# Moving the spatial bias of a gated unit from TensorE to VectorE, and reordering the unit's stages

## The chip, the core and the metric

The kernel runs on one core of one Trainium2 chip. The metric is device time in microseconds (us) of one execution. A core has five engines that run side by side, each through its own queue in order: TensorE (PE, matmuls; its weight loads are shown as PEld), VectorE (DVE), ScalarE (ACT), GpSimd (POOL) and SyncE (SP, which here only issues DMAs). Matmul results land in PSUM, everything else lies in SBUF.

## The reference

Attention with grouped heads, whose output x goes straight into a gated MLP with a spatial projection (batch B = 8, sequence S = 384, 16 query heads on 4 key/value heads, D = 64, model width 1024, d_ff 1024):

```python
attn = softmax(scale * q @ k.T)                  # per head, 384 x 384
x = (attn @ v).transpose(0, 2, 1, 3).reshape(B, S, 1024)
h = np.maximum(x @ w_in, 0.0)
u, v = h[..., :512], h[..., 512:]
v_n = (v - mean(v)) / np.sqrt(var(v) + 1e-06)    # over the 512 features
v_s = np.einsum('ts,bsd->btd', w_spatial, v_n) + b_spatial[None, :, None]
gated = u * v_s
out = (gated @ w_out).astype(np.float32)
```

## The kernel before

**Two streams on TensorE.** The program is written out in steps n, 18 for each batch (`NU = 18`: six units of a query tile and half of the heads, by three key tiles), by a loop over `range(total + 6)`. In each step the loop emits attention work first: `scores(n)` (two pairs of matmuls on a 64-row half each, then one Exp of 128x1024 by ACT; from step 18 on two steps' scores are emitted together at even n) and, in two steps out of three, `weigh(b, m, hh)` (12 small matmuls against v into the PSUM tile `av`, of which there is one buffer, then a reciprocal and a product by DVE, which free it). Then `run_fill(cols)` emits so many matmul columns of the gated unit of an earlier batch. `gated_unit(b)` is a generator that yields the columns of each matmul; it starts at step 18(b+1)+2. So the unit of one batch lies between the attention matmuls of the next, and what is left of the last batch's unit comes alone at the end, the tail.

**The gated unit, in order** (before): three tiles of v (token tile st; `pv` at L322, 8 matmuls of 512 columns; then DVE: relu to `vr` L332, statistics L334, L335); four blocks of u transposed (`pu` at L369, 8 matmuls of 384 columns, relu to `uT` by ACT at L377); the normalisation in two parts (`normal(0)` after block 0: ACT Ln and Exp, L343 and L344, give `rstd`; `normal(1)` after block 1: DVE makes `nmr` at L346 and POOL the three `vn` at L351); four gates (`psp`, m = 0 to 3: one matmul of a vector of ones with the bias at L383, three against the spatial weights at L386, then DVE multiplies PSUM with `uT` into `gT` at L394); then the projection (`po` at L401, 24 matmuls of 512 columns, copied out by DVE and ACT in turn at L410, and stored by SP at L412 and L414). Batch 0 computes u by token tile instead (L303, L312), since its x arrives tile by tile.

**The bias** is a row in fp16 and a second row with its rounding rest, both in `bias_b`, which `prep_spatial` fills on POOL (L431 to L433).

**Buffers and queues.** All PSUM tiles `pv`, `pu`, `psp`, `po` and the transposes share three buffers (`ps_ck`, tag "ck"). POOL's queue holds, in program order, the casts of the k, q and v of a later batch (L159, L175, L164; steps 6 and 7 of a batch's 18, for batches 3 and up) and the `vn`. SP's queue holds loads, transposing DMAs of k, q and x (`x_turn`, L284) and stores. At the start `keep_warm` (L471) puts matmuls without use on TensorE while inputs arrive.

```python
        for m in range(NM):
            psp = ps_ck.tile([P, 512], FP32, name=f"psp_{b}_{m}", tag="ck")
            nc.tensor.matmul(psp[:, 0:S], ones_b, bias_b, start=True, stop=False)
...
            nc.vector.tensor_tensor(gT[:, m, :], psp[:, 0:S], uT[:, m, :], ALU.mult)
```

Of the kernel before, what the change touches and what calls it, by code (L numbers as in the profile page):

```python
# [9 lines left out]
FP32 = mybir.dt.float32  # L10
# [7 lines left out]
def kernel(  # L18
# [125 lines left out]
    ones_b = cst.tile([P, P], FP16, name="ones_b")  # L144
    nc.gpsimd.memset(ones_b, 0.0)
    nc.gpsimd.memset(ones_b[0:1, :], 1.0)
    nc.gpsimd.memset(ones_b[32:33, :], 1.0)
    bias_b = cst.tile([P, S], FP16, name="bias_b")
    nc.gpsimd.memset(bias_b, 0.0)
# [121 lines left out]
    def x_tile(b):  # L271
        if b not in xts:
            xts[b] = att.tile([P, NT, NB, P], FP16, name=f"xt_{b}", tag="xt")
        return xts[b]
# [15 lines left out]


    def gated_unit(b):
        xt = x_tile(b)
        last = b == B - 1
        mv = small.tile([P, NT, 2], FP32, name=f"mv_{b}", tag="mv")
        v_r, v_n = [], []
        uT = moe.tile([P, NM, S], FP16, name=f"uT_{b}", tag="uT")

        def u_tile(st):
            pu = ps_ck.tile([P, NM, P], FP32, name=f"pu_{b}_{st}", tag="ck")  # L300
            for m in range(NM):
                for kt in range(NB):
                    nc.tensor.matmul(  # L303
                        pu[:, m],
                        w_in16[:, kt, m * P : (m + 1) * P],
                        xt[:, st, kt],
                        start=(kt == 0),
                        stop=(kt == NB - 1),
                    )
                    if m < NM - 1 or kt < NB - 1:  # L310
                        yield P
            nc.vector.tensor_scalar(  # L312
                uT[:, :, st * P : (st + 1) * P], pu, 0.0, None, op0=ALU.max
            )
            yield P

        for st in range(NT):
            if st == 2 and b == 0:
                yield from u_tile(0)
            pv = ps_ck.tile([P, 512], FP32, name=f"pv_{b}_{st}", tag="ck")  # L320
            for kt in range(NB):
                nc.tensor.matmul(  # L322
                    pv,
                    xt[:, st, kt],
                    w_in16[:, kt, DH:DFF],
                    start=(kt == 0),
                    stop=(kt == NB - 1),
                )
                if kt < NB - 1:
                    yield 512  # L330
            vr = moe.tile([P, DH], FP32, name=f"vr_{b}_{st}", tag="vr", bufs=4)
            nc.vector.tensor_scalar(vr, pv, 0.0, None, op0=ALU.max)  # L332
            stats = small.tile([P, 6], FP32, name=f"stats_{b}_{st}", tag="stats")
            nc.vector.bn_stats(stats, vr)  # L334
            nc.vector.bn_aggr(mv[:, st, :], stats)  # L335
            v_r.append(vr)
            yield 512
        rstd = small.tile([P, NT], FP32, name=f"rstd_{b}", tag="rstd")
        nmr = small.tile([P, NT], FP32, name=f"nmr_{b}", tag="nmr")

        def normal(part):
            if part == 0:
                nc.scalar.activation(rstd, mv[:, :, 1], AF.Ln, bias=eps_t)  # L343
                nc.scalar.activation(rstd, rstd, AF.Exp, scale=-0.5)  # L344
                return
            nc.vector.scalar_tensor_tensor(  # L346
                nmr, mv[:, :, 0], -1.0, rstd, op0=ALU.mult, op1=ALU.mult
            )
            for st in range(NT):
                vn = moe.tile([P, DH], FP16, name=f"vn_{b}_{st}", tag="vn", bufs=6)  # L350
                nc.gpsimd.tensor_scalar(  # L351
                    vn,
                    v_r[st],
                    rstd[:, st : st + 1],
                    nmr[:, st : st + 1],
                    op0=ALU.mult,
                    op1=ALU.add,
                )
                v_n.append(vn)

        if b == 0:
            normal(0)
            normal(1)
            for st in (1, 2):
                yield from u_tile(st)
        for m in range(NM if b else 0):
            pu = ps_ck.tile([P, 512], FP32, name=f"pu_{b}_{m}", tag="ck")
            for kt in range(NB):
                nc.tensor.matmul(  # L369
                    pu[:, 0:S].rearrange("p (t s) -> p t s", t=NT),  # L370
                    w_in16[:, kt, m * P : (m + 1) * P],
                    xt[:, :, kt],
                    start=(kt == 0),
                    stop=(kt == NB - 1),
                )
                yield S
            nc.scalar.activation(uT[:, m, :], pu[:, 0:S], AF.Relu)  # L377
            if m < 2:
                normal(m)
        gT = moe.tile([P, NM, S], FP16, name=f"gT_{b}", tag="gT")  # L380
        for m in range(NM):
            psp = ps_ck.tile([P, 512], FP32, name=f"psp_{b}_{m}", tag="ck")
            nc.tensor.matmul(psp[:, 0:S], ones_b, bias_b, start=True, stop=False)  # L383
            yield S
            for st in range(NT):
                nc.tensor.matmul(  # L386
                    psp[:, 0:S],
                    v_n[st][:, m * P : (m + 1) * P],
                    wsT16[:, st, :],
                    start=False,  # L390
                    stop=(st == NT - 1),
                )
                yield S
            nc.vector.tensor_tensor(gT[:, m, :], psp[:, 0:S], uT[:, m, :], ALU.mult)  # L394
        rows = out[b].rearrange("(p t) d -> p t d", t=NT)
        for tt in range(NT):
            osb = ops.tile([P, DM], FP32, name=f"osb_{b}_{tt}", tag="osb")
            for half in range(2):
                po = ps_ck.tile([P, 512], FP32, name=f"po_{b}_{tt}_{half}", tag="ck")
                for m in range(NM):  # L400
                    nc.tensor.matmul(  # L401
                        po,
                        gT[:, m, tt * P : (tt + 1) * P],
                        w_out16[:, m, half * 512 : (half + 1) * 512],
                        start=(m == 0),
                        stop=(m == NM - 1),
                    )
                    yield 512
                cols = slice(half * 512, (half + 1) * 512)
                (nc.scalar.copy if half else nc.vector.tensor_copy)(osb[:, cols], po)  # L410
                if last:
                    nc.sync.dma_start(rows[:, tt, cols], osb[:, cols])  # L412
            if not last:
                nc.sync.dma_start(rows[:, tt, :], osb)  # L414

    HV = NB * 512
    COLS = NT * HV + NM * NB * S + NM * (NT + 1) * S + NT * 2 * NM * 512
# [4 lines left out]
    b32 = cst.tile([1, S], FP32, name="b32")  # L422

    def load_b():
        pool.dma_start(b32, moe_b_spatial.rearrange("(a s) -> a s", a=1))

    def prep_spatial():
        lo32 = cst.tile([1, S], FP32, name="lo32")
        bp = b32.rearrange("a (p t) -> a t p", t=NT)
        hi = bias_b[0:1, :].rearrange("a (t p) -> a t p", t=NT)  # L430
        nc.gpsimd.tensor_copy(hi, bp)  # L431
        nc.gpsimd.tensor_tensor(lo32.rearrange("a (t p) -> a t p", t=NT), bp, hi, ALU.subtract)
        nc.gpsimd.tensor_copy(bias_b[32:33, :], lo32)  # L433
# [27 lines left out]
    def turn_at(n, f, *args):  # L461

        turns.setdefault(n, []).append((f, args))
# [9 lines left out]
    keep_warm(24)  # L473
# [3 lines left out]
    keep_warm(8)  # L477
    q_transposes(0, 0, 0, by_act, by_dve)
    keep_warm(4)
# [19 lines left out]
    turn_at(0, q_transposes, 0, 1, 0, by_dve)  # L499
# [51 lines left out]
    fill = []  # L551
# [3 lines left out]
    def run_fill(cols):  # L555
        nonlocal owed
        owed = owed + cols if fill else 0.0
        while fill and owed > 0:
            try:
                owed -= next(fill[0])  # L560
            except StopIteration:
                fill.pop(0)

    early = 0
    for n in range(total + 6):
# [13 lines left out]
        if n == 10:  # L579
            fill.append(gated_unit(0))  # L580
        if n >= 2 * NU + 2 and (n - 2) % NU == 0 and (n - 2) // NU <= B:
            fill.append(gated_unit((n - 2) // NU - 1))
        if n < NU + 3:

            c = HV / 4 if 10 <= n < 14 else 2 * HV / 5 if 16 <= n else 0
            early += c
            run_fill(c)
        else:
            run_fill((COLS - (early if n < 2 * NU + 2 else 0)) / (NU if n >= 2 * NU + 2 else NU - 1))
    for g in fill:  # L590
        for _ in g:
            pass
# [29 lines left out]
```

## Time and profile before

| what | value |
|---|---|
| time, median of 3 runs (lowest to highest) | 255.3 us (254.73 to 255.41) |
| the profiled execution's own time | 255.16 us |
| its span (first to last instruction) | 253.1 us |
| what lies around the span | 2.06 us |
| granted TensorE clock | 1.0 |
| pv, 192 matmuls, share of the chain that ended last | 17% |
| pu in blocks, 224 matmuls | 15% |
| psp with the spatial weights, 96 matmuls | 6% |
| psp with the bias, 32 matmuls | 2% |
| POOL, busy per batch while casts run | 7.24 us |
| DVE, busy per batch | 15.9 us |
| ACT, busy per batch | 20.7 us |

The profile's busy time of a matmul overlaps the next one's, so that what a matmul costs is read from the chain of waits, which follows the last instruction back to what released it. "Busy per batch" is from windows of one period of the steady stage.

### The profile page before, as it was taken

Reading aid. Unit: us, or ns where it says so; the run is one execution under the profiler, and the core shown is the slowest. Engines: PE = TensorE matmul, PEld = TensorE weight load, DVE = VectorE, ACT = ScalarE, POOL = GpSimd, SP = SyncE. Lnnn points to the kernel's source line nnn. Section 1 sums busy time; section 2 is a strip of 40 time slices with the busy share of each in tenths; the row PEclk is TensorE's granted clock in tenths of the full one; section 3 lists DMA queues with packets and bytes.
Section 4 is the critical chain, followed back from the end, with each engine's and each line's share of the span. In section 5 each row is a group of like instructions: output and inputs, shape, how many; then the busy total and the mean of one; then the engine's idle time right before and its main releaser. Section 6 shows DMA issues by size and latency. Waiting matters only on the chain.

```text
span 253.1 us, 5997 instructions
## 1 busy us (share of the span) xinstructions
PE 244.7 (97%) x2457; PEld 129.1 (51%) x2457; DVE 140.1 (55%) x365; ACT 167.5 (66%) x215; POOL 75.0 (30%) x118
## 2 busy tenths in 40 slices
PE   7998998999999999999999999999999999999993
PEld 6564657534455445544455445544455445554541
DVE  2455776755727465455727465455727465465541
ACT  3896566687686867777686867777686867761311
POOL 4698857721032500261033400451030000200200
PEclk9999999999999999999999999999999999999999
DMA  7999997999179952999299962999174442025006
GB/s 182 266 290 246 285 301 195 313 217 271 65 143 311 270 182 54 201 304 252 98 137 298 248 223 57 236 279 280 60 145 96 139 153 41 3 67 223 3 22 227
DMA packets 73803, 46.71 MB, mean 185 GB/s; under 512 B 48113, under 2 KB 68657, under 8 KB 73777
## 3 DMA queue, kind: packets, MB, share of 16 engines
q1 hardware_dynamic: 68688, 37.63, 59.7%
q0 software_dynamic: 4048, 8.46, 13.5%
q8 instruction: 19, 0.31, 0.5%
q10 hardware_dynamic: 1040, 0.26, 0.5%
q14 instruction: 8, 0.06, 0.1%
HBM read 25.76 MB, written 12.58 MB: 151 GB/s over the span
## 4 chain that ended last, share of the span: by engine, by line
PE 91%; DVE 4%; ACT 2%; issue 1%; POOL 0%; DVEq 0%; POOLq 0%
PE pv L322 17%; PE av L252 16%; PE po L401 15%; PE sc L238 15%; PE pu L369 15%; PE psp L386 6%; PE warm L471 3%; PE psp L383 2%; ACT aT L245 1%; PE pu L303 1%; DVE x L264 1%; PE qps L205 1%; DVE gT L394 1%; DVE stats L334 1%; PE xps L280 1%
## 5 line engine op out<-in xcount | busy, mean ns | idle before, releaser
L245 ACT ACTIVATE aT<-sc 128x1024 f16<-128x1024 f32 x144 | 139.5, 1022 | 55.8 <-PE sc L238 55.6
L252 PEld LDWEIGHTS <-aT 128*128 128x128 f16 x1152 | 43.9, 97 | 29.1 <-DVE vr L332 5.7
L262 DVE RECIPROCAL r<-av 128x4 f32<-128x4 f32 x96 | 17.1, 178 | 67.2 <-PE av L252 67.2
L351 POOL TENSOR_SCALAR vn<-vr,rstd,nmr 128x512 f16<-128x512 f32 x24 | 18.1, 767 | 117.2 <-DVE nmr L346 90.7
L252 PE MATMUL av<-v,aT 128*128 128x65 f16 x1152 | 52.1, 194 | 0.5 <-DVE x L264 0.5
L401 PE MATMUL po<-w_out,gT 128*128 128x512 f16 x192 | 47.9, 379 | 0.4 <-ACT osb L410 0.3
L322 PE MATMUL pv<-w_in,xt 128*128 128x512 f16 x192 | 47.0, 379 | 0.2 <-DVE osb L410 0.2
L238 PE MATMUL sc<-qT,kT 64*128 64x512 f16 x288 | 45.4, 385 | 0.4 <-ACT aT L245 0.2
L264 DVE TENSOR_TENSOR x<-av,r 128x256 f16<-128x256 f32 x96 | 40.7, 424 | 3.3
L369 PE MATMUL pu<-xt,w_in 128*128 128x384 f16 x224 | 41.5, 326 | 0.0
L175 POOL CAST q<-q 128x768 f16<-128x768 f32 (+1 forms) x36 | 25.2, 732 | 15.3 <-DMA q<-in_q_dram 10.0
L369 PEld LDWEIGHTS <-w_in 128*128 128x128 f16 x224 | 20.2, 98 | 13.7 <-issue 2.5
L322 PEld LDWEIGHTS <-xt 128*128 128x128 f16 x192 | 16.6, 97 | 18.0 <-issue 1.9
L401 PEld LDWEIGHTS <-gT 128*128 128x128 f16 x192 | 16.5, 97 | 16.3 <-DVE gT L394 2.2
L394 DVE TENSOR_TENSOR gT<-psp,uT 128x384 f16<-128x384 f32 x32 | 17.7, 556 | 9.9 <-PE psp L386 9.2
L238 PEld LDWEIGHTS <-kT 64*128 64x128 f16 x288 | 9.1, 94 | 26.4 <-issue 24.5
L410 ACT COPY osb<-po 128x512 f32<-128x512 f32 x24 | 14.1, 589 | 12.1 <-PE po L401 12.0
L386 PE MATMUL psp<-wsT,vn 128*128 128x384 f16 x96 | 22.0, 326 | 0.0
L332 DVE TENSOR_SCALAR vr<-pv 128x512 f32<-128x512 f32 x24 | 16.6, 691 | 9.0 <-PE pv L322 8.3
L410 DVE COPY osb<-po 128x512 f32<-128x512 f32 x24 | 16.5, 688 | 6.4 <-PE po L401 6.3
L377 ACT ACTIVATE uT<-pu 128x384 f16<-128x384 f32 x28 | 13.8, 492 | 8.4 <-PE pu L369 8.4
L334 DVE BATCH_NORM_STATS2 stats<-vr 128x6 f32<-128x512 f32 x24 | 16.7, 695 | 0.8
(55 smaller groups left out, 127.8 us busy)
## 6 DMA issues: line engine op xcount, KB each, us to landing
out_dram<-osb SPq DMA_DIRECT2D x21, 512.0 KB, 3.8
q<-in_q_dram SPq DMA_DIRECT2D x10, 768.0 KB, 6.9
q<-in_q_dram POOLq DMA_DIRECT2D x4, 768.0 KB, 10.1
v<-in_v_dram SPq DMA_DIRECT2D x6, 384.0 KB, 8.3
w_in<-in_moe_w_in_dram POOLq DMA_DIRECT2D x4, 512.0 KB, 9.7
k<-in_k_dram SPq DMA_DIRECT2D x5, 384.0 KB, 4.1
out_dram<-osb SPq DMA_DIRECT2D x6, 256.0 KB, 2.0
q<-in_q_dram SPq DMA_DIRECT2D x2, 512.0 KB, 7.0
```

What stands on the lines that cost most here:

```text
L175: f(q16s[b, j][:, lo:hi, :, hh, :], src[:, hh, lo:hi])
L238: nc.tensor.matmul(sc[:, hh], kTs[b][half, j, t * P : (t + 1) * P], qTs[b, j][half, qt], start=True, stop=True,)
L245: nc.scalar.activation(aTs[b, m][:, t], sc, AF.Exp, scale=scale)
L252: nc.tensor.matmul(av[:, i, :], aTs[b, m][:, t, hh, i * P : (i + 1) * P], v1[b % 2][:, 2 * j + hh, t, 0 : D + 1], start=(t == 0), stop=(t ...
L264: nc.vector.tensor_tensor(x16s[b][:, qt, blk : blk + 2].rearrange("p k (i d) -> p (k i) d", i=2), av[:, :, 0:D], r.to_broadcast([P, G, D]) ...
L322: nc.tensor.matmul(pv, xt[:, st, kt], w_in16[:, kt, DH:DFF], start=(kt == 0), stop=(kt == NB - 1),)
L334: nc.vector.bn_stats(stats, vr)
L369: nc.tensor.matmul(pu[:, 0:S].rearrange("p (t s) -> p t s", t=NT), w_in16[:, kt, m * P : (m + 1) * P], xt[:, :, kt], start=(kt == 0), stop ...
L386: nc.tensor.matmul(psp[:, 0:S], v_n[st][:, m * P : (m + 1) * P], wsT16[:, st, :], start=False, stop=(st == NT - 1),)
L394: nc.vector.tensor_tensor(gT[:, m, :], psp[:, 0:S], uT[:, m, :], ALU.mult)
L401: nc.tensor.matmul(po, gT[:, m, tt * P : (tt + 1) * P], w_out16[:, m, half * 512 : (half + 1) * 512], start=(m == 0), stop=(m == NM - 1),)
L410: (nc.scalar.copy if half else nc.vector.tensor_copy)(osb[:, cols], po)
```

## The change

The bias matmuls go, and with them the tile of ones and the fp16 bias rows. The bias row is loaded broadcast to 128 partitions, and `prep_spatial` is one POOL copy into a tile `bias_b` in fp32. A gate is now three matmuls; DVE adds the bias on reading PSUM, into a tile `g` in fp32, and POOL multiplies `g` with `uT` (DVE does it for gates 1 and 3 of the last batch).

The unit is split into generators of its parts, and one generator `stream` chains them. For batches 1 to 6 the order is: v tiles 1 and 2, the four blocks of u, the four gates, v tile 0 **of the next batch**, the projection. The normalisation is emitted in one piece, both parts, after the fourth matmul of u block 0 (in batch 0: before the second block of u tile 1). In the last batch gates 0 and 1 come ahead of u block 3. The last half row of the output is cut into two pieces of 256 columns, each with its own copy and store. The stream of batch 1 starts at step 40 instead of 38, and each step emits 2304 columns instead of 2389. At the start the useless matmuls are 27, 4 and 6 instead of 24, 8 and 4, and one transpose of q moves from step 0 to step 1.

```diff
-    ones_b = cst.tile([P, P], FP16, name="ones_b")
-    nc.gpsimd.memset(ones_b, 0.0)
...
+    bias_b = cst.tile([P, S], FP32, name="bias_b")
...
+    def normal(b):
+        rstd = small.tile([P, NT], FP32, name=f"rstd_{b}", tag="rstd")
+        nmr = small.tile([P, NT], FP32, name=f"nmr_{b}", tag="nmr")
+        nc.scalar.activation(rstd, mvs[b][:, :, 1], AF.Ln, bias=eps_t)
+        nc.scalar.activation(rstd, rstd, AF.Exp, scale=-0.5)
+        nc.vector.scalar_tensor_tensor(
+            nmr, mvs[b][:, :, 0], -1.0, rstd, op0=ALU.mult, op1=ALU.mult
+        )
+        v_ns[b] = []
         for st in range(NT):
...
+    def u_tile(b, st):
...
+                if st == 1 and m == 1 and kt == 0:
+                    normal(b)
...
+    def u_block(b, m):
+        pu = ps_ck.tile([P, 512], FP32, name=f"pu_{b}_{m}", tag="ck")
+        for kt in range(NB):
...
+            if m == 0 and kt == 3:
+                normal(b)
+            if kt < NB - 1:
+                yield S
+        nc.scalar.activation(uT_tile(b)[:, m, :], pu[:, 0:S], AF.Relu)
+        yield S
+
+    def gate(b, m):
...
+        psp = ps_ck.tile([P, 512], FP32, name=f"psp_{b}_{m}", tag="ck")
+        for st in range(NT):
+            nc.tensor.matmul(
+                psp[:, 0:S],
+                v_ns[b][st][:, m * P : (m + 1) * P],
+                wsT16[:, st, :],
+                start=(st == 0),
+                stop=(st == NT - 1),
+            )
...
+        g = moe.tile([P, S], FP32, name=f"g_{b}_{m}", tag="g", bufs=4)
+        nc.vector.tensor_tensor(g, psp[:, 0:S], bias_b, ALU.add)
+        by = nc.vector if b == B - 1 and m % 2 else nc.gpsimd
+        by.tensor_tensor(gTs[b][:, m, :], g, uTs[b][:, m, :], ALU.mult)
+        yield S
+
+    def project(b, tt, half):
...
+        cuts = (512, 768, 1024) if last and tt == NT - 1 and half else (512 * half, 512 * half + 512)
+        for i, (lo, hi) in enumerate(zip(cuts, cuts[1:])):
...
+            (nc.scalar.copy if half and not i else nc.vector.tensor_copy)(
+                osb[:, lo:hi], po[:, 0 : hi - lo]
+            )
+            if last:
+                nc.sync.dma_start(rows[:, tt, lo:hi], osb[:, lo:hi])
...
+    def stream():
+        for b in range(B):
+            last = b == B - 1
+            if b == 0:
+                yield from v_tile(0, 0)
+                yield from v_tile(0, 1)
+                yield from u_tile(0, 0)
+                yield from v_tile(0, 2)
+                yield from u_tile(0, 1)
+                yield from u_tile(0, 2)
+            else:
+                yield from v_tile(b, 1)
+                yield from v_tile(b, 2)
                 for m in range(NM):
+                    yield from u_block(b, m)
+                    if last and m == 2:
+                        yield from gate(b, 0)
+                        yield from gate(b, 1)
+            for m in range(2 if last else 0, NM):
+                yield from gate(b, m)
             if not last:
+                yield from v_tile(b + 1, 0)
+            for tt in range(NT):
+                for half in range(2):
+                    yield from project(b, tt, half)
...
-    COLS = NT * HV + NM * NB * S + NM * (NT + 1) * S + NT * 2 * NM * 512
+    COLS = NT * HV + NM * NB * S + NM * NT * S + NT * 2 * NM * 512
...
-        pool.dma_start(b32, moe_b_spatial.rearrange("(a s) -> a s", a=1))
+        pool.dma_start(b32, moe_b_spatial.rearrange("(a s) -> a s", a=1).to_broadcast([P, S]))
...
+        pool.tensor_copy(
+            bias_b.rearrange("q (t p) -> q t p", t=NT), b32.rearrange("q (p t) -> q t p", t=NT)
+        )
...
-    keep_warm(24)
+    keep_warm(27)
...
-    keep_warm(8)
+    keep_warm(4)
     q_transposes(0, 0, 0, by_act, by_dve)
-    keep_warm(4)
+    keep_warm(6)
...
-    turn_at(0, q_transposes, 0, 1, 0, by_dve)
+    turn_at(1, q_transposes, 0, 1, 0, by_dve)
...
+        elif n < 2 * NU + 4:
+            run_fill((4 * HV + NM * NT * S + 6 * NM * 512) / (NU + 4 - 3))
         else:
-            run_fill((COLS - (early if n < 2 * NU + 2 else 0)) / (NU if n >= 2 * NU + 2 else NU - 1))
+            run_fill(COLS / NU)
```

More of the change, by code (lines that the diff above doesn't have):

```diff
@@ L143 @@
         nc.gpsimd.memset(v1[i][:, :, :, D:VW], 1.0)
-    ones_b = cst.tile([P, P], FP16, name="ones_b")
-    nc.gpsimd.memset(ones_b, 0.0)
[L146 to L149, printed above, removed]
+    bias_b = cst.tile([P, S], FP32, name="bias_b")
     k16s, q16s = {}, {}
@@ L288, in x_turn @@
         )
[L292 to L313, printed above, removed]
-            )
-            yield P
-        for st in range(NT):
-            if st == 2 and b == 0:
-                yield from u_tile(0)
-            pv = ps_ck.tile([P, 512], FP32, name=f"pv_{b}_{st}", tag="ck")
+    mvs, v_rs, v_ns, uTs, gTs, osbs = {}, {}, {}, {}, {}, {}
@@ new lines, in v_tile @@
+    def v_tile(b, st):
+        if st == 0:
+            mvs[b] = small.tile([P, NT, 2], FP32, name=f"mv_{b}", tag="mv")
+            v_rs[b] = []
+        pv = ps_ck.tile([P, 512], FP32, name=f"pv_{b}_{st}", tag="ck")
+        for kt in range(NB):
+            nc.tensor.matmul(
+                pv,
+                x_tile(b)[:, st, kt],
+                w_in16[:, kt, DH:DFF],
+                start=(kt == 0),
+                stop=(kt == NB - 1),
+            )
+            if kt < NB - 1:
+                yield 512
+        vr = moe.tile([P, DH], FP32, name=f"vr_{b}_{st}", tag="vr", bufs=4)
+        nc.vector.tensor_scalar(vr, pv, 0.0, None, op0=ALU.max)
+        stats = small.tile([P, 6], FP32, name=f"stats_{b}_{st}", tag="stats")
+        nc.vector.bn_stats(stats, vr)
+        nc.vector.bn_aggr(mvs[b][:, st, :], stats)
+        v_rs[b].append(vr)
+        yield 512
@@ new lines, in normal @@
+    def normal(b):
[7 more added lines that the diff above has]
+        v_ns[b] = []
+        for st in range(NT):
+            vn = moe.tile([P, DH], FP16, name=f"vn_{b}_{st}", tag="vn", bufs=6)
+            nc.gpsimd.tensor_scalar(
+                vn,
+                v_rs[b][st],
+                rstd[:, st : st + 1],
+                nmr[:, st : st + 1],
+                op0=ALU.mult,
+                op1=ALU.add,
+            )
+            v_ns[b].append(vn)
@@ L321, in gated_unit, with uT_tile @@
+    def uT_tile(b):
+        if b not in uTs:
+            uTs[b] = moe.tile([P, NM, S], FP16, name=f"uT_{b}", tag="uT")
+        return uTs[b]
+    def u_tile(b, st):
+        pu = ps_ck.tile([P, NM, P], FP32, name=f"pu_{b}_{st}", tag="ck")
+        for m in range(NM):
             for kt in range(NB):
+                if st == 1 and m == 1 and kt == 0:
+                    normal(b)
                 nc.tensor.matmul(
-                    pv,
-                    xt[:, st, kt],
-                    w_in16[:, kt, DH:DFF],
+                    pu[:, m],
+                    w_in16[:, kt, m * P : (m + 1) * P],
+                    x_tile(b)[:, st, kt],
@@ L328, in gated_unit @@
                 )
[L329 to L347, printed above, removed]
-            )
[L349 to L357, printed above, removed]
-                )
-                v_n.append(vn)
@@ L361, in gated_unit @@
[L361 to L399, printed above, removed]
-                for m in range(NM):
[L401 to L412, printed above, removed]
+                if m < NM - 1 or kt < NB - 1:
+                    yield P
@@ new lines, in u_tile @@
+        nc.vector.tensor_scalar(
+            uT_tile(b)[:, :, st * P : (st + 1) * P], pu, 0.0, None, op0=ALU.max
+        )
+        yield P
+    def u_block(b, m):
+        pu = ps_ck.tile([P, 512], FP32, name=f"pu_{b}_{m}", tag="ck")
+        for kt in range(NB):
+            nc.tensor.matmul(
+                pu[:, 0:S].rearrange("p (t s) -> p t s", t=NT),
+                w_in16[:, kt, m * P : (m + 1) * P],
+                x_tile(b)[:, :, kt],
+                start=(kt == 0),
+                stop=(kt == NB - 1),
+            )
+            if m == 0 and kt == 3:
+                normal(b)
+            if kt < NB - 1:
+                yield S
+        nc.scalar.activation(uT_tile(b)[:, m, :], pu[:, 0:S], AF.Relu)
+        yield S
@@ new lines, in gate @@
+    def gate(b, m):
+        if m == 0:
+            gTs[b] = moe.tile([P, NM, S], FP16, name=f"gT_{b}", tag="gT")
+        psp = ps_ck.tile([P, 512], FP32, name=f"psp_{b}_{m}", tag="ck")
+        for st in range(NT):
+            nc.tensor.matmul(
+                psp[:, 0:S],
[4 more added lines that the diff above has]
+            )
+            if st < NT - 1:
+                yield S
[3 more added lines that the diff above has]
+        by.tensor_tensor(gTs[b][:, m, :], g, uTs[b][:, m, :], ALU.mult)
+        yield S
@@ new lines, in project @@
+    def project(b, tt, half):
+        last = b == B - 1
+        rows = out[b].rearrange("(p t) d -> p t d", t=NT)
+        if half == 0:
+            osbs[b, tt] = ops.tile([P, DM], FP32, name=f"osb_{b}_{tt}", tag="osb")
+        osb = osbs[b, tt]
+        cuts = (512, 768, 1024) if last and tt == NT - 1 and half else (512 * half, 512 * half + 512)
+        for i, (lo, hi) in enumerate(zip(cuts, cuts[1:])):
+            po = ps_ck.tile([P, 512], FP32, name=f"po_{b}_{tt}_{half}_{i}", tag="ck")
+            for m in range(NM):
+                nc.tensor.matmul(
+                    po[:, 0 : hi - lo],
+                    gTs[b][:, m, tt * P : (tt + 1) * P],
+                    w_out16[:, m, lo:hi],
+                    start=(m == 0),
+                    stop=(m == NM - 1),
+                )
+                if m < NM - 1:
+                    yield hi - lo
+            (nc.scalar.copy if half and not i else nc.vector.tensor_copy)(
+                osb[:, lo:hi], po[:, 0 : hi - lo]
+            )
+            if last:
+                nc.sync.dma_start(rows[:, tt, lo:hi], osb[:, lo:hi])
+            elif half:
+                nc.sync.dma_start(rows[:, tt, :], osb)
+            yield hi - lo
@@ new lines, in stream @@
+    def stream():
+        for b in range(B):
+            last = b == B - 1
+            if b == 0:
[8 more added lines that the diff above has]
+                yield from v_tile(b, 2)
+                for m in range(NM):
+                    yield from u_block(b, m)
[4 more added lines that the diff above has]
+                yield from gate(b, m)
@@ L413, in gated_unit @@
             if not last:
-                nc.sync.dma_start(rows[:, tt, :], osb)
+                yield from v_tile(b + 1, 0)
+            for tt in range(NT):
+                for half in range(2):
+                    yield from project(b, tt, half)
     HV = NB * 512
-    COLS = NT * HV + NM * NB * S + NM * (NT + 1) * S + NT * 2 * NM * 512
+    COLS = NT * HV + NM * NB * S + NM * NT * S + NT * 2 * NM * 512
     pool, dve = nc.gpsimd, nc.vector
-    b32 = cst.tile([1, S], FP32, name="b32")
+    b32 = cst.tile([P, S], FP32, name="b32")
@@ L424, in load_b @@
     def load_b():
-        pool.dma_start(b32, moe_b_spatial.rearrange("(a s) -> a s", a=1))
+        pool.dma_start(b32, moe_b_spatial.rearrange("(a s) -> a s", a=1).to_broadcast([P, S]))
     def prep_spatial():
[L428 to L432, printed above, removed]
@@ L433, in prep_spatial @@
-        nc.gpsimd.tensor_copy(bias_b[32:33, :], lo32)
+        pool.tensor_copy(
+            bias_b.rearrange("q (t p) -> q t p", t=NT), b32.rearrange("q (p t) -> q t p", t=NT)
+        )
     def load_ws():
@@ L549 @@
                 at(s0 + 3 * m + 5, x_turn, b, 2, 4 * (m - 4), 4 * (m - 3))
-    fill = []
+    fill = stream()
     owed = 0.0
@@ L556, in run_fill @@
         nonlocal owed
[L557 to L564, printed above, removed]
+        owed += cols
+        while owed > 0:
+            owed -= next(fill, 1e9)
     for n in range(total + 6):
@@ L578 @@
             f(*args)
[L579 to L582, printed above, removed]
         if n < NU + 3:
-            c = HV / 4 if 10 <= n < 14 else 2 * HV / 5 if 16 <= n else 0
-            early += c
-            run_fill(c)
-        else:
-            run_fill((COLS - (early if n < 2 * NU + 2 else 0)) / (NU if n >= 2 * NU + 2 else NU - 1))
-    for g in fill:
-        for _ in g:
-            pass
+            run_fill(HV / 4 if 10 <= n < 14 else 2 * HV / 5 if 16 <= n else 0)
+        elif n < 2 * NU + 4:
+            run_fill((4 * HV + NM * NT * S + 6 * NM * 512) / (NU + 4 - 3))
+        else:
+            run_fill(COLS / NU)
+    for _ in fill:
+        pass
     assert not todo and not turns
```

## The prediction

> **What bounds the kernel now.** I read the page's busy shares first, then its chain of waits by engine, then the windows of a period, and last the chain in order of time at the gates, at the end of attention and in the tail.
>
> ```profile
> span 253.1 us, 5997 instructions
> PE 244.7 (97%) x2457; PEld 129.1 (51%) x2457; DVE 140.1 (55%) x365; ACT 167.5 (66%) x215; POOL 75.0 (30%) x118
> ...
> PE 91%; DVE 4%; ACT 2%; issue 1%; POOL 0%; DVEq 0%; POOLq 0%
> ```
>
> PE is busy for 97% and makes 91% of the chain. Windows cut at one point of the period (columns: stretch, length, PE, PEld, DVE, ACT, POOL busy with counts, clock, DMA share, GB/s) show it full in the steady stage:
>
> ```profile
> 91.90:120.38 28.48, 28.48 (x277) 14.11 (x276) 15.95 (x42) 20.69 (x28) 7.24 (x10) 1.00 0.88 185
> 120.38:148.85 28.47, 28.47 (x277) 14.12 (x276) 15.95 (x42) 20.68 (x28) 7.24 (x10) 1.00 0.89 218
> ```
>
> Nothing but PE is near its limit there, so each PE instruction removed shortens the period, as long as no new wait appears. The chain in order of time (start, length, what) prices them:
>
> ```profile
> 133.04 0.16 PE psp L383
> 133.20 0.49 PE psp L386 x3
> 133.69 0.16 PE psp L383
> ```
>
> **The bias matmuls.** L383 costs 0.16 us each. Batches 0 to 6 have 28 of them: 28 x 0.16 = **-4.5 us**. Batch 7's four lie in the tail and are counted there. The later start of the stream and the smaller share per step move no work in or out: when the loop ends, 110 x 2304 = 253440 columns are done of 6 x 41472 + 37376 = 286208, so 32768 are left, against 7 x 43008 - 112 x 2389.3 = 33450 before.
>
> **The bias on DVE, the product on POOL.** The add has the shape of the old product (PSUM and SBUF, 128x384): 0.56 us by the DVE row below, so a PSUM buffer is held no longer. The product is not in the trace. The rows nearest to it:
>
> ```profile
> L394 DVE TENSOR_TENSOR gT<-psp,uT 128x384 f16<-128x384 f32 x32 | 17.7, 556 | 9.9 <-PE psp L386 9.2
> L159 POOL CAST k<-k 128x384 f16<-128x384 f32 x14 | 6.7, 510 | 16.9 <-DMA k<-in_k_dram 12.3 <-issue 4.6
> L432 POOL TENSOR_TENSOR lo<-b,bias_b 1x384 f32<-1x384 f32 x1 | 1.0, 1030 | 0.1
> L431 POOL CAST bias_b<-b 1x384 f16<-1x384 f32 x1 | 0.7, 692 | 0.0
> L444 POOL CAST ws<-ws 128x384 f16<-128x384 f32 x3 | 2.0, 705 | 0.0
> ```
>
> Below, it costs what a one-input copy of that length does, 0.51; above, two strided copies, 2 x 0.705 = 1.41. One partition or 128 makes no difference (692 against 705 ns), so L432, with two inputs, is nearest: I take 1.0 us.
>
> Is it hidden? Steps by the columns: in the step before the gates' main part (r = 13 of 18) PE does av 0.48, then gate 0 until 0.81, gate 1 until 1.30, one matmul of gate 2; step 14: scores 0.54, gate 2 until 2.33, gate 3 until 2.81; then v tile 0 of the next batch, 8 x 0.215, with av, scores and av between, until 6.1, when the projection starts. It reads gate 3 as its fourth matmul, 6.75. DVE: r and x of av until 1.14, adds end at 1.66, 2.2, 2.94, 3.5. POOL starts at 1.75 and with 1.0 + 0.05 each ends gate 3 at 5.95. Spare 0.8 us: no stall, **0**. The cover is the v tile alone: without it the projection would start at 2.9 and wait some 3 us in each of 7 batches. At 1.41 us a product ends at 7.6 and PE waits 0.9 x 7 = 6.5 us: that is the upper end.
>
> The Trainium skill speaks against this move ("GPSIMD Engine Reference", section on performance versus the Vector engine): two-input elementwise work is about twice as slow there, 4497 ns for 2048 fp32 elements. In proportion that would be an estimated 0.84 us here, less than my 1.0, and the sum would stay the same, because of the cover.
>
> POOL's queue: the products stand behind the vn and ahead of the next batch's casts, which ran at 163.60 to 173.2, from the gates on. They now start some 3 us later. Those behind them on SP, the turns of k and q, come nearly a batch later, so 0. The products add 4 us to POOL's 7.24 in 28.
>
> **The moved v tile.** It needs x tile 0 of the next batch, whose transposing DMA is emitted at step 8 and lands in 3.3 us (5.3 at most); v starts at step 14.9, some 10 us later: 0. In batch 0 the DMA starts at 41.52 and v at about 49: 0. Broadcasting the bias (197 KB instead of 1.5 KB) stands behind the loads on POOL's queue and is used after 45 us: 0; POOL's two bias steps dropped there (1.03 + 0.49) ended long before the vn: 0.
>
> **The normalisation in one piece** puts a wait into DVE's queue. The stretch of before:
>
> ```profile
> 156.80 0.31 ACT L343 ACTIVATE rstd<-mv,eps_t 128x3 f32<-128x3 f32 x1
> 157.14 0.21 ACT L344 ACTIVATE rstd<-rstd 128x3 f32<-128x3 f32 x1
> ...
> 157.38 0.16 DVE L346 SCALAR_TENSOR_TENSOR nmr<-mv,rstd 128x3 f32<-128x3 f32 x1 [0.46 <-ACT rstd L344]
> 157.71 2.27 POOL L351 TENSOR_SCALAR vn<-vr,rstd,nmr 128x512 f16<-128x512 f32 x3 [12.96 <-DVE nmr L346]
> ```
>
> There DVE waited 0.46 us. Now, counted from the end of v tile 2: three u matmuls 0.49, the pair of scores of step 8, its Exps 0.85 to 2.79 (1.94 a pair), Ln and Exp until 3.23, nmr until 3.42. DVE is done with the statistics at 1.68 and stands for 1.6 us. Behind nmr are r and x of step 9, ready at 2.5, which end at 3.97 and free the one av buffer; PE asks for it at 2.0 + 0.48 + 0.97 + 0.54 = 4.0. A tie: between 0 and 0.5 us a batch. I take 0.05 x 6 = **+0.3** (0 to +3.0). In batch 0 such a stop is there already (chain of DVE and ACT at 37.25 to 40.2): +-0.3, taken as 0.
>
> **End of attention.** From 222.13 to 230.60 the chain holds po 5.16, scores 0.54, four av 1.92, transposes 0.44, together 8.06 of 8.47 us; the rest is PE waiting for a copy that ACT does after two Exps. The projection of batch 6 moves behind the last scores: -0.4 to 0, **-0.2**.
>
> **The tail.** Before, in the chain:
>
> ```profile
> 241.14 0.16 PE psp L383
> 241.31 0.49 PE psp L386 x3
> ...
> 243.85 0.57 DVE gT L394
> ...
> 244.47 4.72 PE po L401 x21
> 249.19 0.02 issue
> 249.21 0.58 ACT osb L410
> ```
>
> From the end of the last v tile, 235.94, to 249.19 it takes 13.25 us. In the changed kernel gate 0 comes after three u blocks, 24 x 0.1625 = 3.9 us. The vn don't come sooner:
>
> ```profile
> 238.71 2.26 POOL L351 TENSOR_SCALAR vn<-vr,rstd,nmr 128x512 f16<-128x512 f32 x3 [21.79 <-PE pu L369]
> ```
>
> They end 3.5, 4.3 and 5.0 us after 235.94, so gate 0 waits 0.85. Gate 2 then ends at 7.5, gate 3 at 8.0; the add of gate 2 at 8.16, POOL's product at 9.3. The projection has used gates 0 and 1 by 8.43 and waits 0.9 for gate 2. Work: 5.2 + 12 x 0.1625 + 5.16 = 12.3; with the waits 14.05 to 14.4, against 13.25: **+0.95** (between -0.65, the bias matmuls alone, and +1.5).
>
> Another rule of the skill bears on this place ("SBUF — State Buffer", "Who interferes with whom"): a DVE instruction with two SBUF inputs and a GpSimd one that reads SBUF exclude each other. No row of before shows such a pair. By it DVE's product of gate 3 would begin only when POOL's of gate 2 has ended, and the tail would be 0.35 longer.
>
> The last piece: 256 columns copied by DVE (0.42, the row of x with 256) instead of 0.58 by ACT, and 128 instead of 256 KB, which moved at some 380 GB/s: -0.16 - 0.35, and 0.1 back for the extra store's issue: **-0.4** (0 to -0.7).
>
> **Start.** The first 24 matmuls of no use took 2.74, 0.114 each: three more +0.34, four fewer -0.43, two more +0.21: **+0.1** (0 to +0.35). The transpose moved to step 1 precedes scores that ACT takes up 1 us later: 0.
>
> **Sum:** -4.5 + 0.3 - 0.2 + 0.95 - 0.4 + 0.1 = -3.75, on the profiled execution's 255.16 (span 253.1 and 2.06 around it; 0.14 under the median of 255.3): 251.4, taken as **251.5 us**.
>
> **Rivals.**
> - *The tail doesn't lose.* For it: gates 0 and 1 are done under u block 3. Against: the ends of the vn above. The tail's term is -0.65 instead of +0.95: 249.9.
> - *DVE held at nmr.* For it: the tie above, and the av buffer is single. Against: PE never waited there before. At 0.25 to 0.5 a batch, +1.5 to +3 instead of 0.3: 252.7 to 254.2.
> - *Slower: the products come late.* The place is the first matmuls of each projection that read gates 2 and 3. Stall begins at (6.75 - 0.1 - 1.75) / 4 = 1.22 us from product to product, and it eats the gain from about 0.53 a batch, 1.36 apart; at 1.46 it gives 258. For it: no row shows a POOL product of 128 partitions in two types. Against: L432 at 1.03.
>
> **How the numbers follow.** Forecast (250.5 to 252.6) 0.55; tail without loss 0.15; DVE held 0.18, of which 0.04 ends within 0.3% of before; late products 0.10; rest 0.02. A measurement of this kernel tells 0.3% (0.8 us) from no change. Faster 0.85, same 0.05, slower 0.10. The range takes both neighbours in but their last part: 249.6 to 254.0.
>
> **What would show it.** L383 gone and the period at 27.8 us with PE full; POOL's product row at 0.9 to 1.1 us and no wait of po for gT in the steady stage; nmr waiting over 1 us for rstd, and av waiting for x at step 10, or not; in the tail a wait of psp for vn of 0.85 and of po for gT of 0.9. A product over 1.3 us, or a period over 28.2, would make the prediction wrong.

## The result

The changed kernel takes 253.16 us (median of 4 runs, 252.91 to 253.19) against 255.36 for the kernel before (also 4 runs here, one more than in the table above), a ratio of 0.9912 (95% interval 0.9887 to 0.9937): 2.2 us faster, inside the range of 249.6 to 254.0. The forecast was 251.5, so of a gain of 3.75 us some 2.0 came (profiled executions 255.16 and 253.12).

The page of the changed kernel:

```profile
span 251.3 us, 6020 instructions
...
PE 240.9 (96%) x2430; PEld 125.7 (50%) x2430; DVE 139.7 (56%) x368; ACT 168.2 (67%) x215; POOL 98.3 (39%) x142
...
PE 87%; DVE 7%; issue 1%; ACT 1%; POOL 1%; POOLq 0%; DVEq 0%
```

PE's share of the chain fell from 91% to 87%, DVE's rose from 4% to 7%: part of what PE no longer does, it now waits for DVE. In the chain in order of time the added DVE rows lie in the first 60 us, at the end of attention (222 to 226) and ahead of the tail (231 to 235). In a steady period the chain holds PE alone, and a wait shows there only as an av that takes longer. The new operations, from the groups by shape (busy, mean ns, idle before):

```profile
L392 POOL TENSOR_TENSOR gT<-g,uT 128x384 f16<-128x384 f32 x30 | 26.5, 914 | 29.4 <-DVE g L390 29.4
...
L390 DVE TENSOR_TENSOR g<-psp,bias_b 128x384 f32<-128x384 f32 x32 | 16.4, 552 | 5.9 <-PE psp L380 5.9
...
L392 DVE TENSOR_TENSOR gT<-g,uT 128x384 f16<-128x384 f32 x2 | 1.8, 880 | 0.2
```

One period of the steady stage, cut from step 14 to step 14 (columns as before):

```profile
105.74:133.80 28.06, 28.03 (x275) 13.65 (x276) 15.57 (x42) 20.82 (x27) 10.60 (x14) 1.00 0.83 207
```

The period went from 28.47 to 28.06: 0.42 us instead of the 0.645 of the four matmuls. The chain in order of time shows where the rest stays, at the av of steps 7 and 10:

```profile
93.34 0.48 PE av L247 x12
93.82 1.08 PE pv L294 x5
94.89 0.02 issue
94.92 0.55 PE av L247 x12
...
99.36 0.56 PE sc L233 x4
99.92 0.54 PE av L247 x12
```

An av behind other matmuls costs 0.38 to 0.48 here; these two cost 0.55 and 0.54, with a gap ahead. What they wait for, in the timeline of DVE and PE:

```profile
92.70 0.69 DVE L304 TENSOR_SCALAR vr<-pv 128x512 f32<-128x512 f32 x1 [1.16 <-PE pv L294]
...
93.42 0.69 DVE L306 BATCH_NORM_STATS2 stats<-vr 128x6 f32<-128x512 f32 x1
...
94.25 0.15 DVE L257 RECIPROCAL r<-av 128x4 f32<-128x4 f32 x1
94.44 0.42 DVE L259 TENSOR_TENSOR x<-av,r 128x256 f16<-128x256 f32 x1
...
94.92 0.55 PE L247 MATMUL av<-v,aT 128*128 128x65 f16 x12
...
99.14 0.16 DVE L316 SCALAR_TENSOR_TENSOR nmr<-mv,rstd 128x3 f32<-128x3 f32 x1 [1.45 <-ACT rstd L315]
```

The statistics of v tile 1 stand ahead of r and x of step 6 on DVE, x ends at 94.86, and the one av buffer comes free only then. The nmr at 99.14 stops DVE for 1.45 us, as the prediction had it.

Cutting both traces at the scores of the same steps splits the gain (in us, changed minus before): -0.4 by step 10; -0.5 by step 44 (the first -0.4 included), so batch 0's gates brought next to nothing; -2.5 from step 44 to step 142; -0.1 from there to the end of the last v tile; **+1.3 in the tail** (from there to the last po, 14.55 instead of 13.23); -0.1 behind it. Together, before rounding, -1.8 in the span. Another 0.24 lies outside it: around the span are 1.82 us in the changed kernel's profiled execution, 2.06 in that of before. All runs of the old order on record have 1.96 to 2.08 there and all of the new one 1.73 to 1.85, with the bias matmuls or without. What in the new order does this was not looked for.

### The profile page after: what moved, and what is told of

Its sections match the earlier page's. It is cut to its first block, busy times and chain, and to the rows that moved or that the text cites. A ratio compares the mean times of both kernels' runs of the same rounds, so it can differ in the third digit from the quotient of the medians.

```text
span 251.3 us, 6020 instructions
## 1 busy us (share of the span) xinstructions
PE 240.9 (96%) x2430; PEld 125.7 (50%) x2430; DVE 139.7 (56%) x368; ACT 168.2 (67%) x215; POOL 98.3 (39%) x142
## 4 chain that ended last, share of the span: by engine, by line
PE 87%; DVE 7%; issue 1%; ACT 1%; POOL 1%; POOLq 0%; DVEq 0%
PE av L247 17%; PE pv L294 16%; PE sc L233 15%; PE po L406 15%; PE pu L361 13%; PE psp L380 6%; PE warm L504 3%; DVE stats L306 2%; DVE vr L304 2%; DVE x L259 2%; PE pu L344 1%; PE qps L200 1%; ACT aT L240 1%; POOL vn L322 1%; PE xps L275 1%
## 5 line engine op out<-in xcount | busy, mean ns | idle before, releaser
L294 PE MATMUL pv<-w_in,xt 128*128 128x512 f16 x192 | 49.5, 378 | 0.0
L406 PE MATMUL po<-w_out,gT 128*128 128x512 f16 (+1 forms) x196 | 48.2, 375 | 0.9 <-POOL gT L392 0.9
L392 POOL TENSOR_TENSOR gT<-g,uT 128x384 f16<-128x384 f32 x30 | 26.5, 914 | 29.4 <-DVE g L390 29.4
L415 DVE COPY osb<-po 128x512 f32<-128x512 f32 (+1 forms) x25 | 16.8, 671 | 11.6 <-PE po L406 11.6
L415 ACT COPY osb<-po 128x512 f32<-128x512 f32 (+1 forms) x24 | 13.9, 580 | 12.4 <-PE po L406 12.3
L380 PE MATMUL psp<-wsT,vn 128*128 128x384 f16 x96 | 19.6, 326 | 0.6 <-POOL vn L322 0.6
L390 DVE TENSOR_TENSOR g<-psp,bias_b 128x384 f32<-128x384 f32 x32 | 16.4, 552 | 5.9 <-PE psp L380 5.9
```

Of the source, the lines that this page charges most:

```text
L294: nc.tensor.matmul(pv, x_tile(b)[:, st, kt], w_in16[:, kt, DH:DFF], start=(kt == 0), stop=(kt == NB - 1),)
L380: nc.tensor.matmul(psp[:, 0:S], v_ns[b][st][:, m * P : (m + 1) * P], wsT16[:, st, :], start=(st == 0), stop=(st == NT - 1),)
L392: by.tensor_tensor(gTs[b][:, m, :], g, uTs[b][:, m, :], ALU.mult)
L406: nc.tensor.matmul(po[:, 0 : hi - lo], gTs[b][:, m, tt * P : (tt + 1) * P], w_out16[:, m, lo:hi], start=(m == 0), stop=(m == NM - 1),)
L415: (nc.scalar.copy if half and not i else nc.vector.tensor_copy)(osb[:, lo:hi], po[:, 0 : hi - lo])
```

## The experiments

**The start.** The kernel before with the changed start alone, and with the first count left at 24:

```diff
-    keep_warm(24)
+    keep_warm(27)
...
-    keep_warm(8)
+    keep_warm(4)
...
-    keep_warm(4)
+    keep_warm(6)
...
-    turn_at(0, q_transposes, 0, 1, 0, by_dve)
+    turn_at(1, q_transposes, 0, 1, 0, by_dve)
```

> The kernel before with only the changed start (27, 4 and 6 useless matmuls, one transpose of q a step later). If the start is what brought the scores forward by 0.39 us, the first Exp begins at 6.7 instead of 7.16 and the time falls by 0.4 us to 254.9. Rival: the start is worth nothing (as the prediction's +0.1 has it) and the 0.39 us come from the POOL memsets that the change dropped; then the first Exp stays at 7.1 to 7.3 and the time at 255.2 to 255.5.

> As the run before, but with the first count left at 24 (24, 4, 6). If the gain at the start comes from TensorE having no gap before the transposes of k (27 instead of 24), the gap is back and the first Exp is no earlier than 7.0. Rival: it comes from the shorter second count (4 instead of 8) alone; then the first Exp is at 6.6 to 6.8 here too.

Measured: 255.75 us, ratio 1.0019 (0.9996 to 1.0043), first Exp at 6.39; and 255.23, ratio 0.9995 (0.9981 to 1.0009), first Exp at 6.59. The Exp did begin earlier in both, as the first theory of the first run and the second of the other have it, but the time didn't follow. In profiles of kernels with one and the same start the first Exp lay between 6.34 and 7.05, and with the start of before at 7.16 and 6.25. So where the first Exp lies varies that much under one and the same start, neither theory of its cause is decided, and the -0.4 of the first steps can't be counted as a gain of the change.

**The bias without the move.** The old order, the bias added by DVE and the product on POOL:

```diff
-            nc.tensor.matmul(psp[:, 0:S], ones_b, bias_b, start=True, stop=False)
...
-            nc.vector.tensor_tensor(gT[:, m, :], psp[:, 0:S], uT[:, m, :], ALU.mult)
+            g = moe.tile([P, S], FP32, name=f"g_{b}_{m}", tag="g", bufs=4)
+            nc.vector.tensor_tensor(g, psp[:, 0:S], bias_b, ALU.add)
+            by = nc.vector if last and m % 2 else nc.gpsimd
+            by.tensor_tensor(gT[:, m, :], g, uT[:, m, :], ALU.mult)
```

> The kernel before with the bias part alone: no bias matmuls, add on DVE, product on POOL, v tiles in their old place. If the moved v tile is the cover of POOL's products, the projection waits for the last product: it ends 2.4 us after the last gate and is read 0.65 after it, less attention work between, so 1.3 to 1.8 us in each of 7 batches; less 4.5 for the matmuls: 259 to 263 us. Rival: the products are early enough anyway and the move brings nothing; then 251 to 252.

Measured: 265.75 us, ratio 1.0394 (1.0352 to 1.0435), more than expected. Its chain at the gates:

```profile
139.49 0.61 PE psp L379 x3
...
140.19 0.57 DVE g L388
...
141.78 0.93 POOL gT L390
142.70 0.05 issue
142.75 1.04 PE po L397 x4
```

From the last gate, 140.10, to 142.75 PE waits for the products. The period is 29.73: 0.645 gained and 1.9 lost. The v tile in the changed kernel is the cover, and without it the same edit costs 10 us.

**The move without the bias.** The changed kernel with the bias matmuls and one product on DVE per gate again:

```diff
+        nc.tensor.matmul(psp[:, 0:S], ones_b, bias_b, start=True, stop=False)
+        yield S
...
-        g = moe.tile([P, S], FP32, name=f"g_{b}_{m}", tag="g", bufs=4)
-        nc.vector.tensor_tensor(g, psp[:, 0:S], bias_b, ALU.add)
...
+        nc.vector.tensor_tensor(gTs[b][:, m, :], psp[:, 0:S], uTs[b][:, m, :], ALU.mult)
```

> The changed kernel with the bias matmuls and the one product on DVE put back, everything else as changed. If the new order itself costs 0.23 us a period and something in the tail, this is slower than before: 28.7 a period, 256 to 257.5 us. Rival: the missing part of the gain lies with the add and the POOL product; then the new order is free and this is at 254.7 to 255.3.

Measured: 263.96 us, which neither theory had. The timeline names the cause:

```profile
129.86 0.30 ACT L319 ACTIVATE rstd<-mv,eps_t 128x3 f32<-128x3 f32 x1 [2.36 <-DVE mv L312]
...
131.36 0.49 PE L252 MATMUL av<-v,aT 128*128 128x65 f16 x10 [1.21 <-ACT aT L245]
```

With the bias matmuls a step emits 2389 columns instead of 2304, and so the fourth u matmul, with the normalisation behind it, falls into step 7 instead of 8. There Ln stands ahead of the Exps of step 8 on ACT and holds them until the statistics are done; PE stops 1.2 us for an Exp in each period. So a further kernel has the normalisation one matmul later:

```diff
-            if m == 0 and kt == 3:
+            if m == 0 and kt == 4:
```

> The new order with the bias matmuls again, but with the normalisation one matmul later, so that it falls into step 8, behind its two Exps, as it does in the changed kernel. In the run without this, Ln stood ahead of the Exps of step 8 and ACT waited 2.4 us for the statistics, which gave a period of 29.8. If that was all, the period is 28.47 + 0.2 = 28.7 and the time 256 to 257.5 us. Rival: the order itself costs a microsecond a period when the bias matmuls are there; then 260 us or more.

Measured: 255.3 us, ratio 1.0000 (0.999 to 1.0011), below what I expected. The period is 28.43, so the new order costs nothing by itself, and the wait at step 7 isn't there:

```profile
122.92 1.08 PE pv L299 x5
124.00 0.38 PE av L252 x12
124.37 0.22 PE pv L299
```

The timeline points to the columns again (no run changed them alone): with 2389 a step, two matmuls follow v tile 1 ahead of step 6's scores, with 2304 only one. So vr begins 0.26 us ahead of those scores instead of 0.03, and the statistics are out of the way in time. One matmul of difference in the emission is worth 0.2 us a period there and 1.4 us (29.83 against 28.43) at the normalisation.

**The two waits of DVE, one by one.** First the normalisation of batches 1 to 6 in two parts, then the statistics of v tiles 0 and 1 (batches 1 and up) emitted three matmuls later:

```diff
-            if m == 0 and kt == 3:
-                normal(b)
+            if m == 0 and kt == 3 and b == B - 1:
+                normal(b)
+            elif kt == 3 and m < 2 and b < B - 1:
+                normal(b, m)
```

> The changed kernel with the normalisation of batches 1 to 6 in two parts again, Ln and Exp at u block 0, nmr and vn at block 1. If nmr's wait in DVE's queue (1.45 us) delays the av of step 10, the wait falls under 0.6 and some 0.08 us a period come back: period 27.97 instead of 28.05, time 252.6. Rival: the loss per period lies only with the statistics of the v tile (step 7); then the period stays at 28.05 and the time at 253.1.

```diff
+        if 0 < b and st < NT - 1:
+            late.append([3, statistics])
+        else:
+            statistics()
         yield 512
```

> The changed kernel with the statistics of v tiles 0 and 1 (batches 1 and up) emitted three matmuls later, so that r and x of the weighing at step 6 stand ahead of them on DVE. If DVE's order at the v tile is what makes the av of step 7 wait, that wait goes, the period falls by 0.17 to 27.88 and the time by 1.0 to 1.2 us to 252.0. Rival: nmr alone is the cause; then the period stays at 28.05 and the time at 253.1.

Measured: 253.45 us, ratio 0.9927 (0.99 to 0.9953), for the split. The stretch from step 8 to 16 of each period shrank by 0.08, as expected, but 0.47 were lost at step 36, where PE waits for a transposing DMA of q, and 0.36 at one v tile (at 177 us), and the time tells nothing. For the later statistics: 252.34 us, ratio 0.9881 (0.9848 to 0.9915), the period at 27.85, and the wait gone from its chain:

```profile
121.83 1.08 PE pv L296 x5
122.91 0.37 PE av L247 x12
123.29 0.43 PE pv L296 x2
```

So 0.20 of the 0.225 us that a period fell short came from the statistics. The step in the time, 0.8 us, is in keeping with it, though the intervals against the kernel before overlap.

**All products on DVE.**

```diff
-        by = nc.vector if b == B - 1 and m % 2 else nc.gpsimd
+        by = nc.vector
```

> The changed kernel with every product on DVE. The products (0.45 to 0.56 each, if POOL's product beside them is what made them 0.88 in the tail) stand ahead of r and x of the weighing at step 15, so av of step 16 waits 0.7 to 1.0 us in each period: 258 to 260 us. Rival: DVE, at 55% busy, takes them in without a wait: 252.5 to 253.3, and POOL was not needed.

Measured: 265.64 us, ratio 1.0389 (1.0314 to 1.0465), more than expected. The group of the product and the wait list (us in total, times, longest):

```profile
L392 DVE TENSOR_TENSOR gT<-g,uT 128x384 f16<-128x384 f32 x32 | 19.8, 620 | 3.1
```

```profile
PE av L247 <- DVE x L259: 11.5, 10, 1.8
```

In the chain of a period DVE works through r, x, four adds, four products and r and x again without a pause from 137.82 to 143.79, while av of step 16 waits for the last of them; the period is 29.77. That DVE is busy 56% in the changed kernel says nothing about the stretch in which it takes part in two streams. POOL was needed, though its product takes longer.

**A longer product on POOL**, the prediction's rival on the slower side. Half a product more ahead of each (its result is written over):

```diff
+        if b < B - 1:
+            nc.gpsimd.tensor_tensor(
+                gTs[b][:, m, 0 : S // 2], g[:, 0 : S // 2], uTs[b][:, m, 0 : S // 2], ALU.mult
+            )
```

> The changed kernel with half a product more on POOL ahead of each product of batches 0 to 6 (written over by the whole one). From product to product it takes 1.35 instead of 0.88 us, the last one ends some 0.5 us after the projection needs it, as in the prediction's rival: +0.4 to +0.6 in 7 batches, 256 to 257.5 us. Rival: there is more cover than the sum gave (PE is late itself), then 253.1 to 253.8.

```profile
L396 POOL TENSOR_TENSOR gT<-g,uT 128x384 f16<-128x384 f32 x30 | 27.4, 914 | 4.8 <-DVE g L390 2.6
...
L393 POOL TENSOR_TENSOR gT<-g,uT 128x192 f16<-128x192 f32 x28 | 15.4, 550 | 27.0 <-DVE g L390 27.0
```

Measured: 260.98 us, ratio 1.0207 (1.0166 to 1.0249), more than expected, the period at 29.42. The half product took 0.55, not half of 0.91, so from product to product it was 1.50. The prediction's formula gives 1.75 + 4 x 1.50 + 0.1 - 6.75 = 1.1 us of stall for that; it was 1.37. The rival is real, it begins between 0.91 and 1.5, and the change stays clear of it.

**The tail.** All u blocks ahead of the gates in the last batch, and the first three projections side by side, gates 0 and 1 first:

```diff
-                    if last and m == 2:
-                        yield from gate(b, 0)
-                        yield from gate(b, 1)
...
+        for pair in ((0, 1), (2, 3)):
+            for i in range(3):
...
+                for m in pair:
+                    nc.tensor.matmul(
+                        pos[i],
```

> The changed kernel with another tail: all four u blocks of the last batch ahead of its gates, and the first three projections side by side (gates 0 and 1 of all three, then gates 2 and 3). If the tail lost 0.96 us to psp waiting for vn and 1.05 to po waiting for gT, the time from the end of the last v tile to the last po falls from 14.5 to some 12.7 us and the time to 251.3. Rival: the waits only move (to the first po, which now waits for gate 0's product); then 252.3 to 253.0.

The tail of the changed kernel in its timeline, for comparison, and behind it a product of DVE in the tail of the run with all products on DVE, where POOL has nothing to do:

```profile
237.21 0.34 PE L380 MATMUL psp<-wsT,vn 128*128 128x384 f16 x1 [0.22 <-POOL vn L322]
...
237.96 0.82 PE L380 MATMUL psp<-wsT,vn 128*128 128x384 f16 x4 [0.41 <-POOL vn L322]
...
239.11 0.91 POOL L392 TENSOR_TENSOR gT<-g,uT 128x384 f16<-128x384 f32 x1 [1.21 <-DVE g L390]
239.56 0.89 DVE L392 TENSOR_TENSOR gT<-g,uT 128x384 f16<-128x384 f32 x1
...
242.35 5.13 PE L406 MATMUL po<-w_out,gT 128*128 128x512 f16 x26 [0.86 <-POOL gT L392]
```

```profile
253.93 0.56 DVE L392 TENSOR_TENSOR gT<-g,uT 128x384 f16<-128x384 f32 x1
```

psp waits for the vn and po for POOL's product, both as the prediction had them. Measured for the other tail: 252.92 us, ratio 0.9913 (0.9895 to 0.993); 13.75 us from the last v tile to the last po instead of 14.55, where I expected 12.7. The time is the rival's, and the chain shows the part of the wait that only moved:

```profile
238.60 1.96 PE psp L380 x12
...
241.15 0.56 DVE g L390
241.70 0.04 issue
241.75 1.06 PE po L437 x4
```

The add of gate 2 stands on DVE behind the product of gate 1, and that one takes 0.88 us since POOL's product of gate 0 runs beside it. Of these 0.8 us only 0.24 show in the median; the profiled run began its Exps 0.3 later, and at the scores of step 142, ahead of the tail, it was 0.46 behind the changed kernel's.

**All of it together.** Split normalisation, later statistics, the other tail; first with the last piece stored from ACT's queue, then with every store on SP's:

```diff
-                nc.sync.dma_start(rows[:, tt, lo:hi], osb[:, lo:hi])
+                (nc.scalar if i else nc.sync).dma_start(rows[:, tt, lo:hi], osb[:, lo:hi])
```

> The changed kernel with the split normalisation, the later statistics, the other tail, and the last piece stored from ACT's queue, so that its issue does not stand behind the one before on SP. If the four losses are separate: -0.5, -1.1, -1.8 and -0.3, together 249.4 us. Rival: they overlap (a wait taken away at one step comes back at the next), then 250.3 to 251.3.

> The changed kernel with the split normalisation, the later statistics and the other tail, every store on SP's queue. The run with all four edits had a period of 27.77 us and 13.75 us from the last v tile to the last po, but 4.6 us from there to the end of the span, with the last store on ACT's queue, against 3.9 with SP's. If that store cost the difference, this is at 251.0 us; if the end varies by itself, 251.4 to 251.8.

Measured: 251.64 us, ratio 0.9868 (0.9846 to 0.989), and 251.64 us, ratio 0.9857 (0.9837 to 0.9877): the first is slower than either of its theories had it. The period is 27.77 us in the first, 0.7 under that of before. From the last po to the end of the span it took 4.6 us with the store on ACT's queue, and 4.6 with SP's in the second kernel too, where the other tail alone had 4.0. So the queue isn't the cause; what is stays open. The second kernel's runs spread from 251.17 to 253.56, and the profiled one is the longest. Its chain says why, in part:

```profile
52.16 5.93 DMA qT<-q
58.09 0.14 issue
58.22 0.61 PE sc L233 x4
```

The first scores of batch 2 (step 36) wait 1.65 us for the transposing DMA of its q, 0.69 in the first kernel of the pair. The same line stands in the chain of six of the kernels profiled here, with the scores of that step at 56.00 to 58.22. The other half of the 2.05 us between the two profiled runs was lost by step 8, where a load of q lands only at 13.49. Both medians are 1.5 us under the changed kernel's; against the kernel before, the interval of the second lies just clear of the changed kernel's, that of the first just overlaps it. Their edits are the losses found above.

## Why the prediction was nearly right

- **What bounds the kernel**: right. PE is full in the period (28.03 of 28.06, a busy time in which the waits below don't show, since an av that waits only overlaps the matmul before it less), and with the waits taken away the four matmuls bring 0.66 to 0.7 us a period (28.43 or 28.47 to 27.77).
- **The bias on DVE, the product on POOL**: right. 0.552 against 0.56 taken for the add, 0.914 against 1.0 for the product; four products end before the projection starts, and no po waits for gT in the steady stage. The estimate from the Trainium skill's page "GPSIMD Engine Reference" (section on performance versus the Vector engine), 0.84, was nearer below than mine above. "The cover is the v tile alone" is shown by the run without it.
- **The moved v tile, "0"**: its DMA, its x tile and its queues cost nothing, as said. What I left out is DVE: with the new number of columns a step, the statistics of v tile 1 fall just ahead of r and x. This is the step of the prediction that failed, its condition for the price of the matmuls, "as long as no new wait appears": 0.2 us x 6, some 1.2 us. I had walked through DVE's order at nmr and at the gates, and not at the v tiles.
- **The normalisation in one piece**: the mechanism was right (DVE held 1.45 us against the 1.6 worked out, av of step 10 late), and the price, 0.05 a period, was 0.08.
- **Batch 0**: I counted its four matmuls in full. By step 44 they are not to be seen. The chain there shows the same order on DVE, with v tile 0 of batch 1 between the products and the projection:

```profile
51.78 0.70 DVE vr L304
...
52.51 0.71 DVE stats L306
...
53.52 0.43 DVE x L259
53.95 0.05 issue
54.00 0.54 PE av L247 x12
```

  PE stands 0.44 us idle ahead of that av, by the timeline, and 0.64 in all between the scores of steps 28 and 44, against 0.10 before. The transposing DMA of q isn't in the chain of either kernel there. The first of the six waits above (step 43) lies in this stretch too. Equal steps are also not equal work: by step 44 the changed kernel has put out three u matmuls (0.49 us) fewer, so the loss up to there is nearer 1 us than 0.5, and it wasn't taken apart further.
- **The tail**: mechanism right, size short: +1.3 instead of +0.95. The waits were 0.96 (0.85 said) and 1.02 (0.9 said; the 0.86 of the timeline counts from the modelled end of the matmul before), and 0.2 more for gate 3, whose product on DVE took 0.88 us beside POOL's, against 0.56 alone in the tail of the run with all products on DVE. This is the pair of which the Trainium skill's page "SBUF — State Buffer", "Who interferes with whom", says that they exclude each other; the trace goes the same way, with 0.32 us more where the two overlap for 0.46.
- **The end**: -0.4 expected, -0.1 measured (3.96 us from the last po to the end before, 3.86 after). The smaller copy (0.42) and the smaller store are there, but the store's issue stands behind that of the piece before and ends 0.73 us after its copy, 0.36 before.
- **The end of attention**: -0.2 expected, -0.1 measured (12.20 us from the scores of step 142 to the last v tile before, 12.13 after).
- **The start**: +0.1 expected, nothing measurable in the two runs of it alone.

That the time came within 1.7 us of the forecast is in part luck. In this pair of profiles the first steps gave 0.4 us, which varies under one and the same start, and 0.24 came outside the span, of which the prediction says nothing; without these two the losses listed here are some 2.3 us.

## What to carry to other kernels

Where an order is written out in columns or steps, an edit that changes the columns moves every other instruction against it, and a wait of a full microsecond can come or go with one matmul: after such an edit walk through the in-order queue of each helper engine at every buffer of which there is one, not only at the place edited. A slower engine may take work off a bound one for nothing, if there is other work for the bound one between the product and its use; without that work the same edit lost 10 us. Compare an order alone only after its phase has been set again, or the comparison measures the phase.

## What was not expected of the hardware

- DVE's product of two SBUF tensors took 0.88 us where POOL's ran beside it, and 0.56 without.
- A POOL product of half the columns took 0.55 us, where the whole one takes 0.91.
- The first Exp of one and the same start lay between 6.34 and 7.05 us, and the two kernels with the start alone (6.39 and 6.59) were not faster for it.
- What lies around the span is 1.73 to 1.85 us in all runs of the new order and 1.96 to 2.08 in all of the old one.
